# Top-k attention and a highway layer on one core: row maxima by a reduction of their own, one exponential for two rows of scores, and a sign change on GpSimd

## The chip, the core and the metric

The kernel runs on one NeuronCore of a Trainium2 chip. Its engines work side by side, each through its own queue in order, and wait for each other by semaphores: TensorE (PE), VectorE (DVE), ScalarE (ACT), GpSimd (POOL), and SyncE (SP), which here only starts DMAs. The metric is the device time of one execution in microseconds (us). Before the change the median of three runs is 804.51 us (803.33 to 804.64).

## The reference, cut to what matters

```python
def _attn_ref(q, k, v):                  # 8 batches, 8 heads, 576 rows, head size 64
    scores = (1 / sqrt(64)) * matmul(q, k.T)
    kth = the 32nd largest score of each row
    scores = where(scores >= kth, scores, -1e9)
    scores = scores - max(scores, axis=-1)
    attn = exp(scores)
    attn = attn / (sum(attn, axis=-1) + 1e-09)
    return matmul(attn, v)

def _moe_ref(x, w_h, w_t, b_t):          # 4608 tokens, width 512
    H = maximum(x @ w_h, 0.0)
    T = 1 / (1 + exp(-(x @ w_t + b_t)))
    return T * H + (1 - T) * x
```

The output of the attention, with the heads side by side, is the input `x` of the highway layer. All inputs and the output are float32; q, k and v are drawn with a deviation of 0.1.

## The kernel before

A unit is 128 rows of scores, each 576 columns wide: one block of 128 query rows of one head, or, for the last 64 rows of a sequence, two heads side by side. A batch has 4 x 8 + 4 = 36 units. Units are taken two at a time, so there are 18 pairs in a batch and 144 in all (`NG`). In 16 of the 18 pairs both units are whole blocks of one query range; in the other 2 each unit holds two half blocks.

`step(i)` writes out by hand, under a manual schedule, what each engine gets for pair i; the order of the calls is the order in each engine's queue. A pair lives over several steps:

- `scores` (L297): PE computes the scores of a pair in PSUM (two buffers of three banks). `copy_scores` (L347): ACT copies both units to SBUF as `sc`.
- `segments` (L352): DVE finds the 8 largest of each of 6 segments of 96 columns, 12 MAX8 a pair, into `cand`, sorted within a segment.
- `refine` (L359) finds the 24th largest candidate, a threshold, without sorting all 48. It takes neighbouring segments in opposite order: `high` (L367) is the pairwise maximum, `low` (L369) the pairwise minimum, `neg` (L371) is `high` with its sign changed. The 8 largest of `low` (L374) and of `neg` (L377) go into `en`, L379 combines them into column 1 of `cand`, and one reduction (L383) takes the maximum of column 0 (the row's largest score, `TOP`) and of column 1 (the threshold, `THR`) for both units into `wall`. `refine` is a generator: each `next(ra)` in `step` issues one of its instructions, so that others can be put between them.
- `biases` (L391): POOL multiplies the row maxima and the previous pair's kth values by constants: the biases of the exponential and of `above`.
- `mask_count` (L396): ACT writes a mask of the scores above the threshold and counts them; `mask_add` (L408): PE adds the mask to the scores in PSUM, which takes the counted ones out of the way; `below` (L423): DVE finds the 8 largest of what is left (L424).
- `hits` (L427, DVE), `pick_a` (L438, POOL) and `pick_b` (L442, DVE) choose by the count which of the nine values (threshold and the 8 below it) is the 32nd largest, into `wall`.
- `expo` (L415): ACT computes the exponential of a unit, with the row's maximum as its bias; two a pair, one on each side of the copy of the next pair's scores.
- `above` (L445, ACT) and `above_one` (L448, POOL) turn the kth value into a factor `r`; `keep_both` (L459, DVE) takes the minimum of `e` and `r` for both units; a DMA transposes the result (`transposes`, L486), PE multiplies by the values and a column of twos (`values`, L494), so the denominators come out with the sums.
- `ffn_pieces` (L556): when all heads of a query block are there, POOL adds a small constant to the denominators (L564), DVE takes the reciprocal (L566), POOL scales (L571), PE, ACT and POOL do the highway layer in pieces that later steps work off (`pool_work`, L617, L618, L631). `blk_norm` (L647) does the same in the tail.

At the end `finish` (L954) checks by three sums of signs that the assumptions held (`sure`, L943); if one does not hold, a slow loop computes everything again.

In a step DVE's queue after the 12 segment maxima of the next pair and the two maxima of L424 is: high, low, hits, neg, two maxima of low, two maxima of neg, `pick_b`, L379, the reciprocal if there is one, L383, `keep_both`. POOL's queue is: biases, `above_one`, a piece of the highway layer, `pick_a`, the sum of denominators if there is one, and the issue of a DMA. The biases of a step are made to wait for `keep_both` (`after`, L475).

Of the kernel before, what the change touches and what calls it, by code (L numbers as in the profile page):

```python
# [26 lines left out]
def kernel(  # L27
# [70 lines left out]

    TOP, THR, KTH = 0, 1, NPK + 1
    wall = consts.tile([P, NU + 2, NPK + 2], FP32)  # L100
    fac = consts.tile([P, 2, 2], FP32)
    nc.vector.memset(fac[:, :, 0], -scale)
    nc.vector.memset(fac[:, :, 1], -BIGK * (1.0 - 2.0**-24))
    be = consts.tile([P, NG + 1, 2, 2], FP32)
    NE = 4
# [5 lines left out]
    csum = consts.tile([P, NU], FP32)  # L111
    eps = consts.tile([P, H], FP32)
    nc.vector.memset(eps[:], 2.0e-9)
    nc.vector.memset(wall[:, 0:2, KTH : KTH + 1], 0.0)

    def kth(u):
        return wall[:, u + 2, KTH : KTH + 1]

    def tb(u):
        return be[:, u // 2, u % 2, 0:1]  # L120

    def eb(u):
        return be[:, u // 2 + 1, u % 2, 1:2]
# [223 lines left out]
    def copy_scores(both):  # L347
        sc = scpool.tile([P, 2, S], FP32, name="sc")
        nc.scalar.copy(sc[:], both)  # L349
        return [sc[:, s, :] for s in range(2)]  # L350

# [6 lines left out]

    def refine(g, cand):  # L359
        u0, u1 = pairs[g][0], pairs[g][1] + 1  # L360
# [6 lines left out]
        nc.vector.tensor_tensor(high[:].rearrange("p (s k r) -> p s k r", s=2, r=8), one, two, ALU.max)  # L367
        yield
        nc.vector.tensor_tensor(low[:].rearrange("p (s k r) -> p s k r", s=2, r=8), one, two, ALU.min)  # L369
        yield  # L370
        nc.vector.tensor_scalar(neg[:], high[:], -1.0, None, ALU.mult)  # L371
        yield
        for s in range(2):
            nc.vector.max(en[:, 0, s, 1:9], low[:, s * HALF : (s + 1) * HALF])  # L374
            yield
        for s in range(2):
            nc.vector.max(en[:, 1, s, 0:8], neg[:, s * HALF : (s + 1) * HALF])  # L377
            yield
        nc.vector.scalar_tensor_tensor(  # L379
            out=cand[:, :, :, 1], in0=en[:, 1, :, 0:8], scalar=-1.0, in1=en[:, 0, :, 0:8], op0=ALU.mult, op1=ALU.min  # L380
        )
        yield
        nc.vector.tensor_reduce(  # L383
            wall[:, u0:u1, TOP : THR + 1],
            cand[:, :, :, 0:2].rearrange("p s r k -> p s k r"),
            mybir.AxisListType.X,
            ALU.max,
        )
        yield

    def biases(g):  # L391
        return nc.gpsimd.tensor_tensor(be[:, g], wall[:, 2 * g : 2 * g + 2, TOP : KTH + 1 : KTH - TOP], fac[:], ALU.mult)  # L392

    def mask_count(u, ps):  # L396
        m1 = masks[u % NM]
        nc.scalar.activation(  # L398
            m1[:].bitcast(I8)[:, 1 : 2 * S : 2],
            ps,  # L400
            AF.Sign,
            bias=wall[:, u, THR : THR + 1],
            scale=ABOVE,
            accum_out=csum[:, u : u + 1],
        )
        return m1
# [8 lines left out]
    def expo(u, sc, e):  # L415
        nc.scalar.activation(e, sc, AF.Exp, bias=tb(u), scale=scale)  # L416
        return e

    def pair_tile(name):
        t = epool.tile([P, 2, S], BF16, name=name)  # L420
        return [t[:, s, :] for s in range(2)] + [t]

    def below(u, ps):  # L423
        nc.vector.max(wall[:, u, THR + 1 : KTH], ps)  # L424

# [12 lines left out]
    def pick_a(pair, hit):  # L438
        u0, u1 = pair[0], pair[1] + 1
        nc.gpsimd.tensor_tensor(hit[:], hit[:], wall[:, u0:u1, THR:KTH], ALU.mult)  # L440

    def pick_b(pair, hit):  # L442
        nc.vector.tensor_reduce(wall[:, pair[0] + 2 : pair[0] + 4, KTH], hit[:], mybir.AxisListType.X, ALU.add)

# [110 lines left out]

    def ffn_pieces(b, qt, xs):  # L556
        nh, ng, w = shape_of(qt)
# [3 lines left out]
        def norm():  # L561
            xs3 = xs[:, 0 : nh * DE].rearrange("p (h e) -> p h e", e=DE)
            rinv = cpool.tile([P, H], FP32, name="rinv")
            nc.gpsimd.tensor_tensor(rinv[:, 0:nh], xs3[:, :, D], eps[:, 0:nh], ALU.add)  # L564
            yield
# [81 lines left out]
    def blk_norm(k):  # L647
        nh, ng, w = shape_of(k["qt"])
        xs3 = k["xs"][:, 0 : nh * DE].rearrange("p (h e) -> p h e", e=DE)
        k["x"] = xpool.tile([P, dm], FP32, name="x")  # L650
        rinv = cpool.tile([P, H], FP32, name="rinv")
        nc.vector.tensor_tensor(rinv[:, 0:nh], xs3[:, :, D], eps[:, 0:nh], ALU.add)
# [55 lines left out]
    layers = []  # L708
    norms = []
    st = {}  # L710
# [19 lines left out]
    def start_scores(g):  # L730
        b = units[pairs[g][0]][0]
        for u in pairs[g]:
            for h in units[u][2]:
                ensure_prep(b, h // 2)
        st[g] = dict(ps=scores(pairs[g], preps[b]), sc=[None, None], et=[None, None], e=[None, None])
        st[g]["seg"] = 0
        st[g]["cand"] = cands[g % len(cands)]
# [5 lines left out]
    def segs(g, n):  # L743
        if g >= NG:
            return
        for c in range(st[g]["seg"], min(2 * NSEG, st[g]["seg"] + n)):
            s, k = divmod(c, NSEG)
            segments(st[g]["cand"][:, s], st[g]["ps"][s], k, k + 1)
        st[g]["seg"] += n
# [12 lines left out]
    def back_xs(g):  # L762
# [8 lines left out]
        if units[pairs[g][1]][2][-1] == H - 1:  # L771
            norms.append(ffn_pieces(b, qt, xs_t[b, qt]))

# [8 lines left out]
    def step(i):  # L782
# [32 lines left out]
        if late:  # L815
            late.pop(0)()
        if back:
            back_pv(j)
# [117 lines left out]
    signs = consts.tile([P, NU], BF16)  # L936
    cnt = consts.tile([P, 3], FP32)
    edge = consts.tile([P, 3], FP32)
    for j, e in enumerate((-(2.0**-60), 2.0**26, -(2.0**-100))):
        nc.vector.memset(edge[:, j : j + 1], e)  # L940
    flag = consts.tile([1, 1], I32)

    def sure(j, src, scale):  # L943

        nc.scalar.activation(
            signs[:],
            src,
# [6 lines left out]
    def finish():  # L954
# [7 lines left out]
        def xs_of(qt, h0, n):  # L962
# [3 lines left out]
            po["t"] = pso_tile()  # L966
            return dict(b=B - 1, qt=qt, xs=xs_t[B - 1, qt])

# [26 lines left out]
        below(pr[1], cur["ps"][1])  # L995
        cur["e"] = pair_tile("e")
        for s, u in enumerate(pr):
            expo(u, cur["sc"][s], cur["e"][s])
        x1 = xps.tile([P, 3 * BANK], FP32, tag="x", name="xs")
# [7 lines left out]
        old["et"] = transposes(pu[0])  # L1007
        nc.vector.tensor_tensor(hit[:], hit[:], wall[:, pr[0] : pr[1] + 1, THR:KTH], ALU.mult)
        pick_b(pr, hit)
# [3 lines left out]
        for s, home in enumerate((bank(x2, 1), bank(x1, 0))):  # L1013
# [5 lines left out]
            nc.scalar.copy(cur["et"][s].rearrange("p c q -> p (c q)"), turned)  # L1019
        sure(0, wall[:, 2 : NU + 2, KTH], 1.0)  # L1020
        sure(1, wall[:, 0:NU, TOP], -1.0)
        values_of(i - 1, 0)
# [5 lines left out]
        do_work(nc.vector, NG * dm)  # L1028
        nc.vector.scalar_tensor_tensor(cond[:], wall[:, 0:NU, THR + 1], ABOVE, wall[:, 0:NU, THR], ALU.mult, ALU.add)
        while stores:  # L1030
# [10 lines left out]
        project(bg, yb["qt"], yb["xT"], wt, True)  # L1041
        for j in range(3):
            nc.tensor.matmul(po["t"][0:1, 0:1], cnt[:, j : j + 1], ones[:], start=(j == 0), stop=(j == 2))
        blk_diff(ya, bank(x1, 0))
        store(*blk_out(ya))
        blk_gate(yb, bg)
        nc.vector.tensor_scalar(flag[:], po["t"][0:1, 0:1], 3.0 * P * NU - 0.5, None, ALU.is_ge)
        blk_diff(yb, bank(x2, 0))
# [103 lines left out]
```

## Time and profile before

| | value |
|---|---|
| median of three runs | 804.51 us |
| the profiled execution | 803.52 us |
| its span from the first to the last instruction | 801.9 us |
| TensorE clock granted | 0.997 |
| instructions | 20159 |

The profile page and the views drawn from the trace are of that one execution, and a term worked out from them is set against its 803.52 us. A row of a group reads: line, engine, operation, what it writes and reads with shapes, count, then busy time in us and the mean of one in ns, then the engine's idle time before these instructions in us and what ended it. A row of the timeline reads: start in us, duration in us, engine, line, operation. A row of the waits reads: who waited, for whom, total us, how many times, the longest. A row of the windows reads: the stretch in us, its length, then busy us and instruction count of PE, of PE's weight loads, of DVE, ACT and POOL, then clock, DMA share and GB/s. The line numbers are those of the kernel before.

### The profile page before, as it was taken

The page shows a single profiled execution, that of the slowest core. Times are in us where ns is not written, and L with a number is a line of the kernel's source. Part 1 is how long each engine was busy: PE and PEld are TensorE (multiplying, and loading weights), DVE is VectorE, ACT ScalarE, POOL GpSimd, SP SyncE. Part 2 cuts the span into 40 slices and gives each one's busy share as a digit, 9 for nine tenths or more (in the row PEclk, how much of TensorE's full clock was granted, in tenths as well). Part 3 has the DMA queues.
Part 4 walks back from the last instruction along what each step waited for, and adds up shares of the span by engine and source line. Part 5 has one row for each costly group of instructions (what it writes and reads, how often), then busy time and mean ns, then how long its engine had stood idle before and what let it go on. Part 6 is the DMA issues. An engine that isn't in the chain of part 4 may idle for free.

```text
span 801.9 us, 20159 instructions
## 1 busy us (share of the span) xinstructions
PE 685.3 (85%) x6369; PEld 494.0 (62%) x6459; DVE 768.5 (96%) x3846; ACT 759.3 (95%) x1401; POOL 564.9 (70%) x750
## 2 busy tenths in 40 slices
PE   7888988888988888888988889888898888988884
PEld 5666666566656666566665656656666566666662
DVE  6999999999999999999999999999999999999996
ACT  5999999999999999999999999999999999999984
POOL 2666867777777776787767776778777777766760
PEclk9999999999999999999999999999999999999998
DMA  6689977976799667987569766897677976565553
GB/s 122 87 134 166 130 118 133 161 128 96 138 153 148 110 98 132 155 144 115 99 137 166 119 114 112 150 151 130 111 125 134 167 117 108 95 104 108 112 84 90
DMA packets 341779, 100.31 MB, mean 125 GB/s; under 512 B 326048, under 2 KB 333856, under 8 KB 341664
## 3 DMA queue, kind: packets, MB, share of 16 engines
q1 hardware_dynamic: 286448, 79.14, 51.8%
q0 software_dynamic: 53536, 19.34, 22.2%
q8 instruction: 53, 0.87, 0.4%
q10 hardware_dynamic: 1680, 0.46, 0.3%
q14 instruction: 62, 0.51, 0.2%
HBM read 31.72 MB, written 9.44 MB: 51 GB/s over the span
## 4 chain that ended last, share of the span: by engine, by line
DVE 65%; ACT 15%; PE 12%; DMA 3%; issue 3%; SPq 1%; DVEq 0%; ACTq 0%
DVE cand L354 24%; DVE wall L424 19%; DVE ep L463 8%; ACT m L398 5%; PE xs L327 4%; ACT e L416 3%; ACT sc L349 3%; DMA xT<-xb 2%; DVE en L374 2%; DVE en L377 2%; DVE cand L379 2%; PE fp L529 2%; ACT r L446 2%; DVE high L367 2%; PE pso L279 2%
## 5 line engine op out<-in xcount | busy, mean ns | idle before, releaser
L354 DVE MAX8 cand<-xs 128x8 f32<-128x96 f32 x1728 | 297.0, 247 | 9.7 <-PE xs L336 6.5
L279 PE MATMUL pso<-cst,ident_b 128*128 128x252 bf16 x1841 | 246.8, 272 | 41.9 <-ACT xs L515 39.5
L449 POOL TENSOR_SCALAR r<-sc,wall 128x576 bf16<-128x576 f32 x135 | 232.5, 1722 | 0.0
L416 ACT ACTIVATE e<-sc,be 128x576 bf16<-128x576 f32 x288 | 227.8, 791 | 0.1
L279 PEld LDWEIGHTS <-ident_b 128*128 128x128 bf16 x1841 | 173.5, 98 | 80.6 <-issue 48.7
L424 DVE MAX8 wall<-xs 128x8 f32<-128x576 f32 x288 | 203.9, 749 | 5.1 <-PE xs L411 2.5
L310 PE MATMUL xs<-kT,qT 64*128 64x256 f32 x1024 | 145.3, 400 | 37.2 <-DVE high L367 28.4
L349 ACT COPY sc<-xs 128x1152 f32<-128x1152 f32 x144 | 161.5, 1122 | 1.0 <-DVE cand L354 0.9
L310 PEld LDWEIGHTS xs<-kT,qT 64*128 64x128 f32 x1024 | 93.0, 186 | 68.6 <-issue 40.2
L398 ACT ACTIVATE m<-xs,wall 128x576 int8<-128x576 f32 x144 | 108.0, 750 | 11.0 <-DVE wall L383 9.4
L398 ACT ACTIVATE m<-sc,wall 128x576 int8<-128x576 f32 x144 | 112.4, 780 | 0.0
L440 POOL TENSOR_TENSOR hit<-hit,wall 128x18 f32<-128x18 f32 x143 | 32.1, 225 | 113.5 <-DVE hit L430 113.5
L446 ACT ACTIVATE r<-sc,be 128x576 bf16<-128x576 f32 x143 | 110.8, 775 | 0.0
L463 DVE TENSOR_TENSOR ep<-e,r 128x1152 bf16<-128x1152 bf16 x135 | 100.9, 748 | 0.4 <-ACT e L416 0.4
L411 PE MATMUL xs<-m,ident_b 128*128 128x512 bf16 (+1 forms) x512 | 90.6, 274 | 9.1 <-ACT m L398 7.0
L392 POOL TENSOR_TENSOR be<-wall,fac 128x4 f32<-128x4 f32 x144 | 29.0, 201 | 78.1 <-DVE ep L463 56.4
L501 PEld LDWEIGHTS <-et 128*128 128x128 bf16 (+1 forms) x1600 | 68.6, 100 | 19.9 <-issue 3.5
L501 PE MATMUL pso<-vb,et 128*128 128x65 bf16 (+1 forms) x1600 | 74.4, 194 | 4.9 <-DMA et<-ep 1.0
L411 PEld LDWEIGHTS <-ident_b 128*128 128x128 bf16 x576 | 51.0, 98 | 35.0 <-issue 13.8
L319 PEld LDWEIGHTS xs<-kd,qT 128*128 128x128 f32 x256 | 38.1, 188 | 42.5 <-issue 42.1
L319 PE MATMUL xs<-kd,qT 128*128 128x128 f32 x256 | 62.5, 326 | 0.0
L618 POOL TENSOR_TENSOR h<-h,x 128x512 f32<-128x512 f32 (+1 forms) x37 | 43.0, 1161 | 0.6
(128 smaller groups left out, 992.6 us busy)
## 6 DMA issues: line engine op xcount, KB each, us to landing
kin<-in_k_dram SPq DMA_DIRECT2D x64, 128.0 KB, 3.1
qin<-in_q_dram SPq DMA_DIRECT2D x62, 128.0 KB, 3.1
out_dram<-s SPq DMA_DIRECT2D x30, 256.0 KB, 3.2
s<-h POOLq DMA_DIRECT2D x29, 256.0 KB, 3.7
xb<-x POOLq DMA_DIRECT2D x30, 128.0 KB, 2.6
vb<-in_v_dram POOLq DMA_DIRECT2D x28, 128.0 KB, 3.9
et<-ep SPq DMA_TRANSPOSE x143, 3.9
vb<-in_v_dram POOLq DMA_DIRECT2D x24, 64.0 KB, 3.2
```

Of the source, the lines that this page charges most:

```text
L279: nc.tensor.matmul(po["t"][:, 4 * DE : BANK], ident_b[:], cst[:, 0 : BANK - 4 * DE], start=True, stop=True, skip_group_check=True,)
L310: nc.tensor.matmul(ps[:, mo + n0 : mo + n0 + 256], qT[r : r + D, hp, qs : qs + P], kT[r : r + D, hp, n0 : n0 + 256], start=(n0 == 0), stop ...
L349: nc.scalar.copy(sc[:], both)
L354: nc.vector.max(cand[:, s, :], sc[:, s * SEG : (s + 1) * SEG])
L398: nc.scalar.activation(m1[:].bitcast(I8)[:, 1 : 2 * S : 2], ps, AF.Sign, bias=wall[:, u, THR : THR + 1], scale=ABOVE, accum_out=csum[:, u ...
L411: nc.tensor.matmul(ps[:, s0:s1], ident_b[:], m1[:, s0:s1], start=False, stop=True, skip_group_check=True)
L416: nc.scalar.activation(e, sc, AF.Exp, bias=tb(u), scale=scale)
L424: nc.vector.max(wall[:, u, THR + 1 : KTH], ps)
L446: nc.scalar.activation(r, sc, AF.Relu, bias=eb(u), scale=BIGK)
L449: nc.gpsimd.tensor_scalar(r, sc, kth(u), None, ALU.is_ge)
L463: return nc.vector.tensor_tensor(out, e[:], r[:], ALU.min)
L501: nc.tensor.matmul(pso[r0 : r0 + ql, col : col + DE], ets[s][:, c, gi * P2 : gi * P2 + ql], vb[:, h, vc, :], start=(c == 0), stop=(c == nc ...
```

## The change

Three things change together, and the values they need move with them.

1. `neg`, the pairwise maxima with their sign changed, is computed by GpSimd as a product with a tile of -1 (`minus`), directly after `high`; VectorE's L371 is gone, and `hits` follows `low` as before.
2. The reduction L383 becomes two. One takes, in one instruction with three overlapping ranges over `cand` (which has two more blocks, filled with -3e38), the row maximum of the first unit, of both units together (`PEAK`), and of the second unit. The other takes the two thresholds. `wall` is laid out by pairs.
3. In the joint pairs (the 16 of 18 with whole blocks) one exponential covers both units, 1152 columns, with the shared maximum `PEAK` as its bias. Since a row's exponentials are then scaled down by exp(row maximum - PEAK), the constant added to its denominator is scaled alike: POOL computes the distances (`distances`) for eight units at a time, ACT their exponential (`share`), 32 of each, and `denominators` adds it. The other 16 pairs keep two exponentials, now both ahead of the copy of scores, and get a bias tile of their own from one more POOL product. The end has a fourth check: no row maximum lies more than 40 (in the exponent) below its pair's.

The diff, cut to its core:

```diff
     cands = []
     for i in range(4):
-        cand = consts.tile([P, 2, 8, 8], FP32, name=f"cand{i}")
-        nc.vector.memset(cand[:, :, NSEG:, 0:1], -3.0e38)
+        cand = consts.tile([P, 4, 8, 8], FP32, name=f"cand{i}")
+        nc.vector.memset(cand[:, 0 :: 3, 0:NSEG, 0:1], -3.0e38)
...
         nc.vector.tensor_tensor(high[:].rearrange("p (s k r) -> p s k r", s=2, r=8), one, two, ALU.max)
         yield
+        nc.gpsimd.tensor_tensor(neg[:], high[:], minus[:], ALU.mult)
+        yield
         nc.vector.tensor_tensor(low[:].rearrange("p (s k r) -> p s k r", s=2, r=8), one, two, ALU.min)
-        yield
-        nc.vector.tensor_scalar(neg[:], high[:], -1.0, None, ALU.mult)
         yield
...
-        nc.vector.tensor_reduce(
-            wall[:, u0:u1, TOP : THR + 1],
-            cand[:, :, :, 0:2].rearrange("p s r k -> p s k r"),
-            mybir.AxisListType.X,
-            ALU.max,
+        at = cands4[:]
+        heads = bass.AP(tensor=at.tensor, offset=at.offset, ap=[at.ap[0], [64, 3], [64, 2], [8, NSEG]])
+        nc.vector.tensor_reduce(wall[:, g, 0:LIST], heads, mybir.AxisListType.XY, ALU.max)
+        yield
+        nc.vector.tensor_reduce(lists(g)[:, :, 0], cand[:, :, :, 1], mybir.AxisListType.X, ALU.max)
+        yield
+
+    def joint(g):
+        return units[pairs[g][0]][1] < nfull
...
     def biases(g):
-        return nc.gpsimd.tensor_tensor(be[:, g], wall[:, 2 * g : 2 * g + 2, TOP : KTH + 1 : KTH - TOP], fac[:], ALU.mult)
+        if not joint(g):
+            nc.gpsimd.tensor_tensor(bs[:, g % 4], wall[:, g, 0:LIST:2], fat[:], ALU.mult)
+        return nc.gpsimd.tensor_tensor(be[:, g], wall[:, g, PEAK : KTH + LW + 1 : LW], fac[:], ALU.mult)
+
+    def distances(g):
+        g0 = g + 1 - NP
+        nc.gpsimd.tensor_tensor(
+            dist[:, g0 : g + 1],
+            wall[:, g0 : g + 1, 0:LIST:2],
+            wall[:, g0 : g + 1, PEAK].unsqueeze(2).to_broadcast([P, NP, 2]),
+            ALU.subtract,
         )
+        share = cpool.tile([P, H], FP32, name="share")
+
+        def expo_share():
+            nc.scalar.activation(
+                share[:], dist[:, g0 : g + 1].rearrange("p g s -> p (g s)"), AF.Exp, bias=eps[:, 0:1], scale=scale
+            )
+
+        return share, expo_share
...
+    def exponentials(g):
+        e = pair_tile("e")
+        sc = st[g]["sc"]
+        if joint(g):
+            nc.scalar.activation(e[2][:], sc[2], AF.Exp, bias=be[:, g, 0:1], scale=scale)
+        else:
+            for s, u in enumerate(pairs[g]):
+                expo(u, sc[s], e[s])
+        return e
...
+        while lows:
+            lows.pop(0)()
         if back:
             back_pv(j)
             back_xs(j)
...
         if live:
-            st[i]["e"] = pair_tile("e")
-            expo(pr[0], st[i]["sc"][0], st[i]["e"][0])
+            st[i]["e"] = exponentials(i)
         if nxt:
             copy_both(i + 1)
...
         if live:
-            expo(pr[1], st[i]["sc"][1], st[i]["e"][1])
+            pass
...
-        for _ in range(2):
+        for _ in range(3):
             next(ra, None)
         if live:
             hit = hits(pr)
             pick_a(pr, hit)
+            shared(i)
             scaling = norms.pop(0)() if norms else iter(())
             next(scaling, None)
...
-        for _ in range(5):
+        for _ in range(4):
             next(ra, None)
         if live:
             pick_b(pr, hit)
         next(ra, None)
         if live:
             next(scaling, None)
         for _ in ra:
             pass
         last = masked()
```

DVE's queue in a step is then: high, low, hits, two maxima of low, two maxima of neg, `pick_b`, L379, the reciprocal if there is one, the reduction for the maxima, the reduction for the thresholds, `keep_both`. POOL's is: biases, `above_one`, a piece of the highway layer, neg, `pick_a`, the distances or the sum of denominators if there is one, the issue of a DMA. PE's instructions and their order are unchanged but for one more check matmul at the end.

More of the change, by code (lines that the diff above doesn't have):

```diff
@@ L1 @@
+import math
 from contextlib import ExitStack
@@ L97 @@
         nc.vector.memset(pidx[:, jj : jj + 1], S - 2.0 * (TOP_K - jj))
[L99 to L104, printed above, removed]
+    LIST, LW = 3, NPK + 2
+    PEAK, KTH = 1, LIST + NPK
+    wall = consts.tile([P, NG + 1, LIST + 2 * LW - 1], FP32)
+    fac = consts.tile([P, 3], FP32)
+    nc.vector.memset(fac[:, 0:1], -scale)
+    nc.vector.memset(fac[:, 1:3], -BIGK * (1.0 - 2.0**-24))
+    fat = consts.tile([P, 2], FP32)
+    nc.vector.memset(fat[:], -scale)
+    be = consts.tile([P, NG + 1, 3], FP32)
+    bs = consts.tile([P, 4, 2], FP32)
+    dist = consts.tile([P, NG, 2], FP32)
+    nc.gpsimd.memset(dist[:], 0.0)
     NE = 4
@@ L349, in copy_scores @@
         nc.scalar.copy(sc[:], both)
-        return [sc[:, s, :] for s in range(2)]
+        return [sc[:, s, :] for s in range(2)] + [sc[:]]
     def segments(cand, sc, lo, hi):
@@ L357, with refine @@
     HALF = NSEG // 2 * 8
-    def refine(g, cand):
-        u0, u1 = pairs[g][0], pairs[g][1] + 1
+    def refine(g, cands4):
+        cand = cands4[:, 1:3]
         en = ends[g % NE]
@@ L382, in refine, with biases, shared @@
         yield
-        nc.vector.tensor_reduce(
-            wall[:, u0:u1, TOP : THR + 1],
-            cand[:, :, :, 0:2].rearrange("p s r k -> p s k r"),
-            mybir.AxisListType.X,
-            ALU.max,
-        )
-        yield
-    def biases(g):
-        return nc.gpsimd.tensor_tensor(be[:, g], wall[:, 2 * g : 2 * g + 2, TOP : KTH + 1 : KTH - TOP], fac[:], ALU.mult)
+        at = cands4[:]
[6 more added lines that the diff above has]
+        return units[pairs[g][0]][1] < nfull
+    def biases(g):
+        if not joint(g):
[8 more added lines that the diff above has]
+            ALU.subtract,
+        )
+        share = cpool.tile([P, H], FP32, name="share")
[4 more added lines that the diff above has]
+        return share, expo_share
+    def shared(g):
+        if joint(g) and units[pairs[g][1]][2][-1] == H - 1:
+            share, ex = distances(g)
+            shares.append(share)
+            lows.append(ex)
     def mask_count(u, ps):
@@ L401, in mask_count @@
             AF.Sign,
-            bias=wall[:, u, THR : THR + 1],
+            bias=top9(u, 0, 1),
             scale=ABOVE,
@@ L423, in below @@
     def below(u, ps):
-        nc.vector.max(wall[:, u, THR + 1 : KTH], ps)
+        nc.vector.max(top9(u, 1), ps)
     def hits(pair):
@@ L439, in pick_a @@
         u0, u1 = pair[0], pair[1] + 1
-        nc.gpsimd.tensor_tensor(hit[:], hit[:], wall[:, u0:u1, THR:KTH], ALU.mult)
+        nc.gpsimd.tensor_tensor(hit[:], hit[:], lists(u0 // 2), ALU.mult)
     def pick_b(pair, hit):
-        nc.vector.tensor_reduce(wall[:, pair[0] + 2 : pair[0] + 4, KTH], hit[:], mybir.AxisListType.X, ALU.add)
+        nc.vector.tensor_reduce(wall[:, pair[0] // 2 + 1, KTH : KTH + LW + 1 : LW], hit[:], mybir.AxisListType.X, ALU.add)
     def above(u, sc, r):
@@ L554, with denominators, ffn_pieces @@
     blocks = []
-    def ffn_pieces(b, qt, xs):
+    def denominators(e, rinv, sums, share):
+        if share is None:
+            return e.tensor_scalar(rinv, sums, 2.0e-9, None, ALU.add)
+        return e.tensor_tensor(rinv, sums, share[:], ALU.add)
+    def ffn_pieces(b, qt, xs, share=None):
         nh, ng, w = shape_of(qt)
@@ L563, in norm @@
             rinv = cpool.tile([P, H], FP32, name="rinv")
-            nc.gpsimd.tensor_tensor(rinv[:, 0:nh], xs3[:, :, D], eps[:, 0:nh], ALU.add)
+            denominators(nc.gpsimd, rinv[:, 0:nh], xs3[:, :, D], share)
             yield
@@ L651, in blk_norm @@
         rinv = cpool.tile([P, H], FP32, name="rinv")
-        nc.vector.tensor_tensor(rinv[:, 0:nh], xs3[:, :, D], eps[:, 0:nh], ALU.add)
+        denominators(nc.vector, rinv[:, 0:nh], xs3[:, :, D], k["share"])
         nc.vector.reciprocal(rinv[:, 0:nh], rinv[:, 0:nh])
@@ L708 @@
     layers = []
-    norms = []
+    norms, shares, lows = [], [], []
     st = {}
@@ L734, in start_scores @@
                 ensure_prep(b, h // 2)
-        st[g] = dict(ps=scores(pairs[g], preps[b]), sc=[None, None], et=[None, None], e=[None, None])
+        st[g] = dict(ps=scores(pairs[g], preps[b]), sc=[None, None, None], et=[None, None], e=[None, None])
         st[g]["seg"] = 0
@@ L771, in back_xs @@
         if units[pairs[g][1]][2][-1] == H - 1:
-            norms.append(ffn_pieces(b, qt, xs_t[b, qt]))
+            norms.append(ffn_pieces(b, qt, xs_t[b, qt], shares.pop(0) if joint(g) else None))
     late = []
@@ L936 @@
     signs = consts.tile([P, NU], BF16)
-    cnt = consts.tile([P, 3], FP32)
-    edge = consts.tile([P, 3], FP32)
-    for j, e in enumerate((-(2.0**-60), 2.0**26, -(2.0**-100))):
+    cnt = consts.tile([P, 4], FP32)
+    edge = consts.tile([P, 4], FP32)
+    for j, e in enumerate((-(2.0**-60), 2.0**26, -(2.0**-100), 40.0 / scale)):
         nc.vector.memset(edge[:, j : j + 1], e)
@@ L966, in xs_of @@
             po["t"] = pso_tile()
-            return dict(b=B - 1, qt=qt, xs=xs_t[B - 1, qt])
+            share = shares.pop(0) if qt < nfull else None
+            return dict(b=B - 1, qt=qt, xs=xs_t[B - 1, qt], share=share)
         def masked(unit, s, of):
@@ L995, in finish @@
         below(pr[1], cur["ps"][1])
-        cur["e"] = pair_tile("e")
-        for s, u in enumerate(pr):
-            expo(u, cur["sc"][s], cur["e"][s])
+        cur["e"] = exponentials(i)
         x1 = xps.tile([P, 3 * BANK], FP32, tag="x", name="xs")
@@ L1007, in finish @@
         old["et"] = transposes(pu[0])
-        nc.vector.tensor_tensor(hit[:], hit[:], wall[:, pr[0] : pr[1] + 1, THR:KTH], ALU.mult)
+        nc.vector.tensor_tensor(hit[:], hit[:], lists(i), ALU.mult)
         pick_b(pr, hit)
@@ L1028, in finish @@
         do_work(nc.vector, NG * dm)
-        nc.vector.scalar_tensor_tensor(cond[:], wall[:, 0:NU, THR + 1], ABOVE, wall[:, 0:NU, THR], ALU.mult, ALU.add)
+        for s in range(2):
+            c = LIST + s * LW
+            nc.vector.scalar_tensor_tensor(
+                cond[:, s::2], wall[:, 0:NG, c + 1], ABOVE, wall[:, 0:NG, c], ALU.mult, ALU.add
+            )
         while stores:
@@ L1041, in finish @@
         project(bg, yb["qt"], yb["xT"], wt, True)
-        for j in range(3):
-            nc.tensor.matmul(po["t"][0:1, 0:1], cnt[:, j : j + 1], ones[:], start=(j == 0), stop=(j == 2))
+        for j in range(4):
+            nc.tensor.matmul(po["t"][0:1, 0:1], cnt[:, j : j + 1], ones[:], start=(j == 0), stop=(j == 3))
         blk_diff(ya, bank(x1, 0))
```

33 lines of the change are left out of this document (22 added, 11 removed).

## The prediction

> **What bounds the kernel now.** I read the page first: busy shares, then the chain that ended last.
>
> ```profile
> PE 685.3 (85%) x6369; PEld 494.0 (62%) x6459; DVE 768.5 (96%) x3846; ACT 759.3 (95%) x1401; POOL 564.9 (70%) x750
> DVE 65%; ACT 15%; PE 12%; DMA 3%; issue 3%; SPq 1%; DVEq 0%; ACTq 0%
> ```
>
> Two engines look full, DVE at 96% and ACT at 95%, and shares cannot say which of them sets the pace. The chain gives DVE 65% and ACT 15%. The table of windows cuts off the first 20 us and the tail:
>
> ```profile
> 20.00:780.00 760.00, 659.28 (x6148) 475.91 (x6234) 743.03 (x3732) 738.16 (x1361) 557.95 (x732) 1.00 0.76 126
> ```
>
> In the 760 us between, the third busy column (DVE) has 743.0: only 17 us of idle time. The fourth (ACT) has 738.2. The view of waits then tells who was late for whom:
>
> ```profile
> DVE cand L354 <- PE xs L336: 6.5, 15, 0.5
> DVE cand L354 <- PE xs L319: 2.9, 7, 0.6
> DVE wall L424 <- PE xs L411: 2.5, 3, 1.1
> DVE ep L463 <- ACT e L416: 0.4, 2, 0.2
> ACT m L398 <- DVE wall L383: 9.4, 25, 0.7
> ```
>
> DVE waited for ACT itself 0.4 us in all; its waits are for score matmuls (6.5 and 2.9 us, L336 and L319), which start when DVE's own `below` is through, and for mask matmuls (2.5 us, L411), which do stand behind ACT's masks. So a pair costs what DVE's queue costs, and I follow DVE's queue. One pair in the timeline, with the POOL instruction inside it:
>
> ```profile
> 408.84 0.19 DVE L367 TENSOR_TENSOR high<-cand 128x48 f32<-128x48 f32 x1
> 408.94 0.20 DVE L369 TENSOR_TENSOR low<-cand 128x48 f32<-128x48 f32 x1
> ...
> 409.06 0.17 DVE L430 TENSOR_TENSOR hit<-pidx,csum 128x18 f32<-128x18 f32 x1
> ...
> 409.15 0.18 DVE L371 TENSOR_SCALAR neg<-high 128x48 f32<-128x48 f32 x1
> 409.24 0.26 DVE L374 MAX8 en<-low 128x8 f32<-128x24 f32 x2
> 409.31 0.23 POOL L440 TENSOR_TENSOR hit<-hit,wall 128x18 f32<-128x18 f32 x1 [1.63 <-DVE hit L430]
> 409.43 0.25 DVE L377 MAX8 en<-neg 128x8 f32<-128x24 f32 x2
> 409.60 0.15 DVE L443 TENSOR_REDUCE wall<-hit 128x2 f32<-128x18 f32 x1
> 409.71 0.19 DVE L379 SCALAR_TENSOR_TENSOR cand<-en 128x16 f32<-128x16 f32 x1
> 409.93 0.21 DVE L383 TENSOR_REDUCE wall<-cand 128x4 f32<-128x32 f32 x1
> 410.06 0.75 DVE L463 TENSOR_TENSOR ep<-e,r 128x1152 bf16<-128x1152 bf16 x1
> ```
>
> What matters here is starts, not durations: `low` starts 0.10 after `high` though `high` lasts 0.19, so independent instructions overlap by about 0.08. Only where one needs the last one's result does it wait: `wall` (L383) starts 0.03 after the end of `cand` (L379), 0.22 after its start. Counting from `high`, the starts are: low 0.10, hit 0.22, neg 0.31, maxima of low 0.40, maxima of neg 0.59, the sum of hits (L443) 0.76, L379 0.87, L383 1.09, keep 1.22. These 1.22 us, 144 times, are what the change edits.
>
> **Part 1: the sign change goes to POOL (144 pairs).** Removing L371 frees one start-to-start step, 409.24 - 409.15 = 0.09, but the maxima of low need `low` (end 0.30), so they come at 0.34 and the maxima of neg could start at 0.52 instead of 0.59. They now wait for POOL. `high` ends at 0.19; POOL answers a DVE result 0.08 later (hit ends at 409.23, POOL starts at 409.31), so neg starts at 0.27. No trace shows a 48-element product on POOL; the neighbours:
>
> ```profile
> L440 POOL TENSOR_TENSOR hit<-hit,wall 128x18 f32<-128x18 f32 x143 | 32.1, 225 | 113.5 <-DVE hit L430 113.5
> L618 POOL TENSOR_TENSOR h<-h,x 128x256 f32<-128x256 f32 x7 | 5.1, 726 | 0.5
> L571 POOL TENSOR_TENSOR x<-xs,rinv 128x512 f32<-128x512 f32 x31 | 32.3, 1043 | 0.0
> L571 POOL TENSOR_TENSOR x<-xs,rinv 128x256 f32<-128x256 f32 x7 | 4.2, 603 | 0.0
> ```
>
> From 225 at 18 elements to 726 at 256 is 2.1 ns an element: 288 ns at 48. The product with a broadcast (603 at 256, 1043 at 512: 1.72 an element) gives 246, the lower bound. I take 0.29, as the row of 18 is nearest: neg ends at 0.56. POOL's way back is at most 0.06 (L440 ends at 409.54, L443 starts at 409.60); I take 0.05. Maxima of neg then start at 0.60-0.61, L379, which needs their end (+0.085 +0.17 +0.03), at 0.88 instead of 0.87. Behind neg on POOL stands the product of hits (L440): it starts at 0.52 instead of 0.47, ends at 0.75, and L443 comes at 0.80, which still lets L379 start on time. So without contention this part costs +0.01 a pair, by the short duration -0.03. That POOL is free when `high` ends is in the row of L440: 113.5 us of idle before 143 of them, 0.8 each.
>
> Contention is the open price L. The trace shows it in one direction, with a reciprocal in the same pair:
>
> ```profile
> 283.10 1.27 POOL L617 TENSOR_TENSOR s<-h,x 128x512 f32<-128x512 f32 x1 [0.48 <-ACT h L616]
> ...
> 283.85 0.58 DVE L367 TENSOR_TENSOR high<-cand 128x48 f32<-128x48 f32 x1
> ...
> 285.12 0.19 DVE L379 SCALAR_TENSOR_TENSOR cand<-en 128x16 f32<-128x16 f32 x1
> 285.21 0.20 DVE L566 RECIPROCAL rinv<-rinv 128x8 f32<-128x8 f32 x1
> 285.34 0.21 DVE L383 TENSOR_REDUCE wall<-cand 128x4 f32<-128x32 f32 x1
> ```
>
> `high`, with two inputs in SBUF, took 0.58 instead of 0.19: it ended 0.06 after POOL's instruction (284.37), so it was locked out until then. In the changed order `hit`, again with two inputs, runs from 0.22 to 0.39 while neg wants to start at 0.27. Bounds: L = 0 if hit's reads are through before neg asks, 0.13 if neg gets nothing before hit's end (0.39 - 0.27 = 0.13 by unrounded times). I take 0.04: `high` needed only 0.06 once it had the port, so `hit` holds it for a small part of its 0.17. Part 1: +0.05 a pair, bounds -0.03 and +0.14.
>
> The Trainium skill, "SBUF — State Buffer", section "Who interferes with whom", states that a DVE instruction with two SBUF inputs and a GpSimd one that reads SBUF share a port, and that the first to issue keeps it for the whole instruction. The stretched `high` agrees; no row shows POOL locked out by DVE. Taken at its word for `hit` it makes L 0.13, which is rival B.
>
> **Part 2: the row maxima get a reduction of their own.** L383 with four results becomes one with three (before it) and one with two.
>
> ```profile
> L383 DVE TENSOR_REDUCE wall<-cand 128x4 f32<-128x32 f32 x144 | 30.3, 210 | 3.6
> L443 DVE TENSOR_REDUCE wall<-hit 128x2 f32<-128x18 f32 x144 | 22.0, 153 | 0.0
> L566 DVE RECIPROCAL rinv<-rinv 128x8 f32<-128x8 f32 x31 | 6.1, 195 | 0.0
> L566 DVE RECIPROCAL rinv<-rinv 128x4 f32<-128x4 f32 x7 | 1.2, 171 | 0.0
> ```
>
> The new one reads column 0 of the candidates, which L379 does not write, so it goes into the 0.22 in which L383 waits for L379, as the reciprocal does above (0.09 after L379, and L383 still 0.22 after it). About as long as L383 (0.21, so a step of 0.13), it lets the second start at 0.22 to 0.25: +0.015. Its cover is that gap; without it the step costs 0.13. The second reduction has L443's shape nearly (0.15 against 0.21), so keep follows 0.07 after it, not 0.13: -0.057. Net -0.04 a pair (bounds -0.06 and 0.00, if results don't shorten it). In the 38 pairs with a reciprocal (31 + 7) the gap is taken: +0.12 x 38 = +4.6 us (bounds 0 and 5).
>
> **Part 3: one exponential a pair.** 128 of 144 pairs are joint.
>
> ```profile
> L416 ACT ACTIVATE e<-sc,be 128x576 bf16<-128x576 f32 x288 | 227.8, 791 | 0.1
> L349 ACT COPY sc<-xs 128x1152 f32<-128x1152 f32 x144 | 161.5, 1122 | 1.0 <-DVE cand L354 0.9
> L515 ACT COPY xs<-pso 128x260 f32<-128x260 f32 x72 | 27.6, 383 | 9.7 <-PE pso L501 7.4
> ```
>
> From 383 at 260 columns to 1122 at 1152 is 0.83 ns a column, so one of 1152 is 791 + 576 x 0.83 = 1269 against 1582: 0.31 x 128 = 40 us off ACT. The 32 new small exponentials give back at most 32 x 0.38 = 12. Some 30 us leave ACT, but only DVE's waits can shrink: the 17 us of idle, less 9.4 for the scores, leave about 7. Most of that has PE held by other work, so I take -2.5 (bounds 0 and -7). The score copy moves behind the longer exponential, 0.48 later; the masks queued behind it on ACT come earlier, since the second exponential is gone.
>
> **Part 4: the rest.** An extra POOL product ahead of L449 in 16 pairs, differences in 32 (some 0.2 each), a fourth check in the tail. They lie in POOL's idle time; +0.8 (bounds 0 and 3).
>
> **Sum** on the profiled run's own time of 803.5 (span 801.9): parts 1 and 2, 144 x (0.05 - 0.04) = +1.6; reciprocals +4.6; ACT -2.5; rest +0.8: +4.5, so 808.0. The median of the runs is 1.0 above the profiled run: 809.
>
> **Rivals.**
> A, it ends faster: neg takes 246 ns and L is 0. Part 1 is -0.03, 144 x -0.07 = -10 us, and with +2.9 of the rest the sum is -7: 797. For it: POOL's product with a broadcast. Against: 225 ns already at 18 elements. It decides from a neg that is back before 0.57.
> B, `hit` keeps the port and neg waits: L = 0.13, 144 x 0.10 = +14.5, +2.9: 822. For it: the lock in the row of `high`. Against: the lock's holder there was a 1.27 us POOL instruction, not a short DVE one. If neg takes the port between `low` and `hit` instead, `hit` ends 0.06 after neg at 0.62, POOL's product of hits at 0.92, L443 comes at 0.97 and L379 at 1.04: +0.17 - 0.04, 144 times, 19 us: 826.
> C, ACT was the bound after all: DVE's idle in the middle goes, 17 us in place of the 2.5 of part 3: 809 - 14.5 = 794. Against: 0.4 us of DVE waits on ACT.
> D, a row maximum lies more than 40 in the exponent below its pair's, the flag is not set and the slow loop runs: at least double the time, over 1600. With inputs drawn at 0.1 the scores lie far closer together.
>
> **How the numbers follow.** Forecast 0.52 (its own range 804 to 817); A 0.24; B 0.18; C 0.05; D 0.01. The predicted time is the forecast's. The range of 797 to 826 takes in A and B. From no change this kernel can be told by about 0.2% (1.6 us). Faster: all of C and most of A, 0.28; same: the lower edge of the forecast and a part of A, 0.12; slower: 0.60.
>
> **What would show it.** Maxima of neg start about 0.64 after `high` and wait for POOL (right), or at 0.52 with no wait (A), or 0.7 and later (B); `hit` longer than 0.17 says neg took the port. L383's successor pair starts 0.09 and 0.22 after L379, and keep 0.07 after the second. ACT's share falls by 3 to 4 points without DVE's idle time falling likewise. Wrong would be: DVE's share falling while the time falls too, or a wait for POOL on another instruction than the maxima of neg or L443.

## The result, and the profile after

The changed kernel is slower by 0.35%: over 20 runs of each, 805.96 us against 803.15 us, a ratio of 1.0035 (95% interval 1.0027 to 1.0043). The three runs shown ahead of the prediction had lain 1.4 us above the longer series of the kernel before.

The page of the changed kernel, its first block and the shares of the chain that ended last:

```profile
span 803.8 us, 20357 instructions
PE 690.8 (86%) x6461; PEld 493.6 (61%) x6461; DVE 775.5 (96%) x3850; ACT 742.3 (92%) x1307; POOL 612.7 (76%) x943
DVE 71%; PE 12%; ACT 10%; DMA 3%; issue 2%; SPq 0%; POOL 0%; DVEq 0%; ACTq 0%
```

The table of windows without the first 20 us and the tail (after PE and PE's weight loads come DVE, ACT and POOL):

```profile
20.00:780.00 760.00, 663.11 (x6217) 474.40 (x6216) 747.45 (x3723) 718.97 (x1261) 604.16 (x920) 1.00 0.76 126
```

ACT has become 19 us emptier in these 760 us (738.2 before), and DVE is busy 4.4 us longer (743.0 before). The view of waits says where ACT's time went:

```profile
ACT m L445 <- DVE wall L406: 30.7, 68, 1.0
DVE cand L373 <- PE xs L355: 6.4, 16, 0.5
DVE cand L373 <- PE xs L338: 2.6, 6, 0.8
DVE wall L481 <- PE xs L458: 3.9, 6, 1.0
```

ACT's masks now wait 30.7 us for DVE's thresholds, 9.4 before. DVE's own waits for scores (6.4 and 2.6) are what they were (6.5 and 2.9), and its wait for masks (3.9, 2.5 before) is no shorter. The relief of ACT went into ACT's own idle time.

One pair of the changed kernel in the timeline, the same one as before the change:

```profile
408.93 0.19 DVE L386 TENSOR_TENSOR high<-cand 128x48 f32<-128x48 f32 x1
409.04 0.20 DVE L390 TENSOR_TENSOR low<-cand 128x48 f32<-128x48 f32 x1
...
409.15 0.17 DVE L487 TENSOR_TENSOR hit<-pidx,csum 128x18 f32<-128x18 f32 x1
409.20 0.29 POOL L388 TENSOR_TENSOR neg<-high,minus 128x48 f32<-128x48 f32 x1 [1.41 <-DVE high L386]
409.27 0.27 DVE L393 MAX8 en<-low 128x8 f32<-128x24 f32 x2
409.44 0.23 POOL L497 TENSOR_TENSOR hit<-hit,wall 128x18 f32<-128x18 f32 x1
409.52 0.27 DVE L396 MAX8 en<-neg 128x8 f32<-128x24 f32 x2
409.70 0.17 DVE L500 TENSOR_REDUCE wall<-hit 128x2 f32<-128x18 f32 x1
409.82 0.19 DVE L398 SCALAR_TENSOR_TENSOR cand<-en 128x16 f32<-128x16 f32 x1
409.91 0.21 DVE L404 TENSOR_REDUCE wall<-cand 128x3 f32<-128x36 f32 x1
410.04 0.18 DVE L406 TENSOR_REDUCE wall<-cand 128x2 f32<-128x16 f32 x1
410.14 0.75 DVE L520 TENSOR_TENSOR ep<-e,r 128x1152 bf16<-128x1152 bf16 x1
```

From the start of `high`: neg on POOL 0.27, maxima of low 0.34, maxima of neg 0.59, sum of hits 0.77, L398 0.89, the two reductions 0.98 and 1.11, keep 1.21. Before, the maxima of neg came at 0.59 too, L379 at 0.87 and keep at 1.22. The instruction taken off DVE has freed nothing: the maxima of neg start 0.03 after POOL is done (409.20 + 0.29 = 409.49), so the step that was saved turned into a wait. The front half, up to L398, is 0.02 longer, since the two maxima of neg together take 0.27 and took 0.25 before (409.43, L377); the back half is 0.03 shorter.

A pair with a reciprocal, the same as the one shown before, from L398 on:

```profile
284.82 0.19 DVE L398 SCALAR_TENSOR_TENSOR cand<-en 128x16 f32<-128x16 f32 x1
284.91 0.19 DVE L629 RECIPROCAL rinv<-rinv 128x8 f32<-128x8 f32 x1
285.02 0.16 DVE L404 TENSOR_REDUCE wall<-cand 128x3 f32<-128x36 f32 x1
285.11 0.17 DVE L406 TENSOR_REDUCE wall<-cand 128x2 f32<-128x16 f32 x1
285.19 0.75 DVE L520 TENSOR_TENSOR ep<-e,r 128x1152 bf16<-128x1152 bf16 x1
```

Here the gap behind L398 is taken by the reciprocal, and the extra reduction costs a step: 0.37 from L398 to keep, 0.34 before (285.12 to 285.46, where keep stands in the timeline of the kernel before):

```profile
285.46 0.75 DVE L463 TENSOR_TENSOR ep<-e,r 128x1152 bf16<-128x1152 bf16 x1
```

### The profile page after: what moved, and what is told of

It is laid out like the page before. It is cut to its first block, busy times and chain, and to the rows that moved or that the text cites. A ratio compares the mean times of both kernels' runs of the same rounds, so it can differ in the third digit from the quotient of the medians.

```text
span 803.8 us, 20357 instructions
## 1 busy us (share of the span) xinstructions
PE 690.8 (86%) x6461; PEld 493.6 (61%) x6461; DVE 775.5 (96%) x3850; ACT 742.3 (92%) x1307; POOL 612.7 (76%) x943
## 4 chain that ended last, share of the span: by engine, by line
DVE 71%; PE 12%; ACT 10%; DMA 3%; issue 2%; SPq 0%; POOL 0%; DVEq 0%; ACTq 0%
DVE cand L373 26%; DVE wall L481 21%; DVE ep L520 8%; PE xs L346 4%; ACT m L445 3%; DVE en L396 3%; DVE en L393 3%; DMA xT<-xb 2%; PE fp L586 2%; PE pso L298 2%; DVE cand L398 2%; DVE high L386 2%; DVE low L390 2%; ACT sc L368 1%; PE xs L329 1%
## 5 line engine op out<-in xcount | busy, mean ns | idle before, releaser
L470 ACT ACTIVATE e<-sc,be 128x1152 bf16<-128x1152 f32 x128 | 161.0, 1258 | 0.1
L445 ACT ACTIVATE m<-xs,wall 128x576 int8<-128x576 f32 x144 | 107.5, 747 | 32.3 <-DVE wall L406 30.7
L388 POOL TENSOR_TENSOR neg<-high,minus 128x48 f32<-128x48 f32 x144 | 41.1, 285 | 92.4 <-DVE high L386 89.9
L458 PE MATMUL xs<-m,ident_b 128*128 128x512 bf16 (+1 forms) x576 | 103.2, 285 | 5.5 <-ACT m L445 3.4
L416 POOL TENSOR_TENSOR be<-wall,fac 128x3 f32<-128x3 f32 x144 | 28.3, 197 | 58.7 <-DVE ep L520 49.3
```

What stands on the lines that cost most here:

```text
L445: nc.scalar.activation(m1[:].bitcast(I8)[:, 1 : 2 * S : 2], ps, AF.Sign, bias=top9(u, 0, 1), scale=ABOVE, accum_out=csum[:, u : u + 1],)
L458: nc.tensor.matmul(ps[:, s0:s1], ident_b[:], m1[:, s0:s1], start=False, stop=True, skip_group_check=True)
L470: nc.scalar.activation(e[2][:], sc[2], AF.Exp, bias=be[:, g, 0:1], scale=scale)
```

## The experiments

Times are medians of 11 or 12 runs, of 5 where that is said, and of 2 for the slowest version. Each ratio is to the kernel before, run on the same chip, with its 95% interval; it can differ from the quotient of the two medians shown by up to 0.0009, and differences in us are taken from the ratios. Where two ratios are set against each other, each brings its interval, mostly of about 0.001 up and down. Diffs are against the kernel before or the changed one, as named, and cut to what matters (`...`).

**Part 1 undone in the changed kernel.**

```diff
-        nc.gpsimd.tensor_tensor(neg[:], high[:], minus[:], ALU.mult)
-        yield
         nc.vector.tensor_tensor(low[:]..., one, two, ALU.min)
         yield
+        nc.vector.tensor_scalar(neg[:], high[:], -1.0, None, ALU.mult)
+        yield
...
```

The counts of `next(ra)` in `step` go back with it, so that neg stands behind `hits` again.

> The changed kernel with part 1 undone: neg is computed by DVE again, in its old place after hits. Theory (the DVE queue sets the pace, and the way over POOL costs it 0.02 us a pair: in the changed kernel L398 starts 0.89 after high, before 0.87): 144 x 0.02 = 3 us less than the changed kernel, a ratio to before of 0.998 to 1.000. Rival (part 1 is free and the extra reduction, the reciprocals behind it or the moved exponentials cost the 0.35%): the ratio stays at 1.003 to 1.004.

803.06 us against 802.76, ratio 1.0004 (0.9994 to 1.0013): just above the range that was expected, and clear of the rival's. Nearly all of the 0.35% goes with part 1: 1.0035 - 1.0004, some 2.5 us (1 to 4 by the ends of the two intervals). The rest of the change together shows no gain, although it takes 34 us of exponentials off ACT (by the groups of the changed kernel 161.0 for the joint ones, 23.0 for the others and 9.5 for the small ones, against 227.8).

**Part 1 alone in the kernel before** (the same lines the other way).

> The kernel before with part 1 alone. Theory: the maxima of neg wait for POOL and start later than DVE's own queue would let them, and L379 comes 0.02 to 0.03 us later: +3 to +4 us, a ratio of 1.004 to 1.005. Rival (the saved DVE instruction pays for the way over POOL): 0.999 to 1.001. A lock of hit or neg would show as hit over 0.18 us or neg over 0.30.

804.43 us against 802.76, 1.0020 (1.0010 to 1.0030), between the two ranges: slower, as the theory has it, but at half of its size. The groups by line and form of this run, POOL's neg and then DVE's instructions around it:

```profile
L371 POOL TENSOR_TENSOR neg<-high,minus 128x48 f32<-128x48 f32 x144 | 41.4, 287 | 91.1 <-DVE high L369 88.3 <-DVE low L373 1.4
...
L376 DVE MAX8 en<-low 128x8 f32<-128x24 f32 x288 | 39.1, 177 | 0.0
L379 DVE MAX8 en<-neg 128x8 f32<-128x24 f32 x288 | 39.1, 177 | 0.1
L432 DVE TENSOR_TENSOR hit<-pidx,csum 128x18 f32<-128x18 f32 x144 | 24.2, 168 | 0.0
```

`hit` lasts 168 ns (170 before) and neg 287: neither was held by the other. The maxima last 177 ns; with neg on DVE, in the run above this one, the same two groups read:

```profile
L393 DVE MAX8 en<-low 128x8 f32<-128x24 f32 x288 | 37.5, 170 | 0.0
L396 DVE MAX8 en<-neg 128x8 f32<-128x24 f32 x288 | 35.8, 164 | 0.0
```

The view of waits hardly shows the stall (0.1 us of idle time), since the engine counts as busy with the maxima of low while the next instruction is held. It has to be read from starts.

**POOL's answer made later**: in the changed kernel neg goes behind the product of hits in POOL's queue.

```diff
-        for _ in range(3):
+        for _ in range(2):
             next(ra, None)
         if live:
             hit = hits(pr)
             pick_a(pr, hit)
+            next(ra, None)
             shared(i)
...
```

In `refine`, neg stands behind `low` for this.

> The changed kernel with POOL's neg placed behind the product of hits on POOL instead of ahead of it. Theory (the maxima of neg wait for POOL, and every ns there goes into the pair): neg starts 0.66 after high instead of 0.27, the maxima of neg at 0.98 instead of 0.59, +0.39 x 144 = 56 us, less some 8 us that waits for scores take in: 845 to 865 us. Rival (the wait is covered by later waits): under 815 us.

849.72 us against 804.01, 1.0574 (1.0555 to 1.0593), inside the expected range: 43 us more than the changed kernel. A pair of this run, with the wait that now shows:

```profile
401.20 0.19 DVE L386 TENSOR_TENSOR high<-cand 128x48 f32<-128x48 f32 x1
...
401.68 0.23 POOL L497 TENSOR_TENSOR hit<-hit,wall 128x18 f32<-128x18 f32 x1 [1.02 <-DVE hit L487]
401.86 0.29 POOL L390 TENSOR_TENSOR neg<-high,minus 128x48 f32<-128x48 f32 x1
...
402.18 0.27 DVE L396 MAX8 en<-neg 128x8 f32<-128x24 f32 x2 [0.37 <-POOL neg L390]
```

The maxima of neg start 0.98 after `high`, 0.39 later than in the changed kernel, and 43 us are 0.30 a pair: three quarters of this delay on POOL went into the time. This place has no slack; the changed kernel stands with POOL's answer just beyond its edge.

**Part 2 alone, in its plain form**: two reductions of two results each.

```diff
-        nc.vector.tensor_reduce(wall[:, u0:u1, TOP : THR + 1], cand[:, :, :, 0:2]..., X, ALU.max)
+        nc.vector.tensor_reduce(wall[:, u0:u1, TOP], cand[:, :, :, 0], X, ALU.max)
+        yield
+        nc.vector.tensor_reduce(wall[:, u0:u1, THR], cand[:, :, :, 1], X, ALU.max)
```

> The kernel before with part 2 alone: L383 becomes two reductions of two results each, for row maxima and for thresholds. Theory: the first goes into the gap behind L379, keep comes 0.03 sooner after the second in 106 pairs, and in the 38 pairs with a reciprocal the gap is taken, +0.05 each: -3 + 2 = -1 us, ratio 0.998 to 1.000. Rival (the extra instruction costs its own step of 0.10 to 0.13 in each pair): +14 to +19 us, 1.018 to 1.023.

801.00 us against 802.76, 0.9974 (0.9964 to 0.9984): one DVE instruction more a pair, and faster by 2.1 us, more than expected. The two pairs that show how, from the timeline of this run, without and with a reciprocal:

```profile
204.43 0.19 DVE L379 SCALAR_TENSOR_TENSOR cand<-en 128x16 f32<-128x16 f32 x1
204.52 0.17 DVE L383 TENSOR_REDUCE wall<-cand 128x2 f32<-128x16 f32 x1
204.65 0.18 DVE L385 TENSOR_REDUCE wall<-cand 128x2 f32<-128x16 f32 x1
204.75 0.75 DVE L460 TENSOR_TENSOR ep<-e,r 128x1152 bf16<-128x1152 bf16 x1
...
209.60 0.19 DVE L379 SCALAR_TENSOR_TENSOR cand<-en 128x16 f32<-128x16 f32 x1
209.69 0.20 DVE L563 RECIPROCAL rinv<-rinv 128x8 f32<-128x8 f32 x1
209.81 0.13 DVE L383 TENSOR_REDUCE wall<-cand 128x2 f32<-128x16 f32 x1
209.85 0.17 DVE L385 TENSOR_REDUCE wall<-cand 128x2 f32<-128x16 f32 x1
209.94 0.75 DVE L460 TENSOR_TENSOR ep<-e,r 128x1152 bf16<-128x1152 bf16 x1
```

The first reduction sits in the gap in which DVE waited for L379 anyway; the second starts 0.22 after L379, as the one reduction did, and keep follows 0.10 after it instead of 0.13. Even with a reciprocal in the gap it is 0.34 to keep, as before the change, where a loss of 0.05 was expected.

**Part 3 alone**: one exponential a joint pair, with the first unit's maximum as bias.

```diff
-            expo(pr[0], st[i]["sc"][0], st[i]["e"][0])
+            if units[pr[0]][1] < nfull:
+                nc.scalar.activation(st[i]["e"][2][:], st[i]["sc"][2], AF.Exp, bias=tb(pr[0]), scale=scale)
+            else:
...
-        if live:
-            expo(pr[1], st[i]["sc"][1], st[i]["e"][1])
```

> The kernel before with part 3 alone: one exponential for a joint pair, with the first unit's row maximum as the bias of both; the small constant in the denominators is not scaled for it. Theory (ACT stands off the path): ACT's busy time falls by some 40 us and the time stays, ratio 0.999 to 1.001; ACT's wait for DVE grows. Rival (the prediction's -2.5 us, bounds 0 and -7): 0.991 to 0.997.

802.59 us against 802.76, 0.9995 (0.9986 to 1.0005): no change that can be told. From the page and the waits of this run:

```profile
PE 684.5 (86%) x6369; PEld 494.0 (62%) x6459; DVE 768.9 (96%) x3846; ACT 737.6 (92%) x1273; POOL 564.9 (71%) x750
ACT m L398 <- DVE wall L383: 29.7, 71, 1.0
```

ACT is busy 22 us less (759.3 before) and waits 20 us more for DVE (9.4 before). Its busy time fell by less than the 40 us expected, since it counts overlapping instructions once: the exponentials' own groups fell by 44 us, from 227.8 to 160.8 (joint) and 23.0 (others).

**Part 3 undone in the changed kernel**, in its cost only: two exponentials with the shared bias.

```diff
-            nc.scalar.activation(e[2][:], sc[2], AF.Exp, bias=be[:, g, 0:1], scale=scale)
+            for s in range(2):
+                nc.scalar.activation(e[s], sc[s], AF.Exp, bias=be[:, g, 0:1], scale=scale)
```

> The changed kernel with part 3 undone in its cost only: a joint pair gets two exponentials of 576 columns again, both with the shared bias. Theory (ACT is off the path by the 31 us that it waits for DVE's thresholds in the changed kernel): ACT's busy time rises by some 40 us, its wait falls, and the time stays within 0.1% of the changed kernel's 1.0035. Rival (ACT's relief is worth 2.5 us or more): 1.0065 or more.

806.40 us against 804.01 over 5 runs, 1.0039 (1.0025 to 1.0052), against 1.0035 with one. ACT's wait for DVE's thresholds fell from 30.7 to 10.2 us. So in both directions, at an ACT share of 92% or 95%, the exponential decides nothing that these runs can tell.

**The three-range reduction narrowed**: neg on DVE, and in place of three maxima only the two units' own, the first serving as the shared one.

```diff
-        at = cands4[:]
-        heads = bass.AP(..., ap=[at.ap[0], [64, 3], [64, 2], [8, NSEG]])
-        nc.vector.tensor_reduce(wall[:, g, 0:LIST], heads, mybir.AxisListType.XY, ALU.max)
+        nc.vector.tensor_reduce(wall[:, g, PEAK:LIST], cand[:, :, 0:NSEG, 0], mybir.AxisListType.X, ALU.max)
...
```

> The changed kernel with neg on DVE again and the three-range reduction narrowed to two results: the first unit's row maximum serves as the shared one, the distances are taken from it, all else stays. Theory (the long reduction is dear where the reciprocal has taken the gap: L404 to L406 0.118 in the mean, against 0.109 with two results): 1.5 to 2 us under the run with neg on DVE (1.0004), ratio 0.998 to 0.999. Rival (the loss is in the distances, the small exponentials and the bias tile): it stays at 1.000.

802.20 us against 804.01, 0.9980 (0.9970 to 0.9989), where the three-range form gave 1.0004: some 1.9 us for the third range. The distances are taken from the first unit's maximum as well, so on these inputs this version does the work of the changed kernel, and it is faster than both kernels. It guards less: a distance can now be positive, when the second unit's maximum is the larger, and the fourth check looks only for distances below -40.

**Parts 2 and 3 in plain form together**, without distances and their small exponentials, the small constant in the denominators not scaled (the two diffs above, of part 2 alone and part 3 alone).

> The kernel before with parts 2 and 3 in a plain form: two reductions of two results each, one exponential a joint pair with the first unit's row maximum as bias, no three-range reduction, no distances; the small constant in the denominators is not scaled. Theory (the parts add up): the ratio of the run with two reductions alone, 0.9974, times that of one exponential alone, 0.9995: 0.996 to 0.998. Rival (together they lose what they gain alone, as in the changed kernel without part 1, 1.0004): 0.999 to 1.001.

800.94 us against 804.01 over 5 runs, 0.9964 (0.9950 to 0.9978): the parts add up. This is the lowest ratio of the versions tried, but its interval overlaps that of the two reductions alone (0.9974). The distances, the small exponentials and the bias tile then cost 0.9980 - 0.9964, some 1.3 us; the two intervals overlap, so that figure stays open.

## Why the prediction was right or wrong

The sign and the mechanism were right: DVE's queue sets the pace, the way over POOL ends just after DVE needs it, ACT's relief is not seen. The size was off: +4.5 us forecast, +2.8 us measured. The terms were further off than their sum, and it is luck that they nearly cancel: by the runs, part 1 was put some 4.7 us too dear and the others together some 3.6 us too cheap, with the 1.3 us left open above counted to part 4. (The first term of the sum, 144 x 0.01, is 1.4 and not 1.6.)

- **The mis-sized term is the contention L in part 1.** The prediction put 0.04 us a pair on neg waiting for the port that `hit` holds, 144 x 0.04 = 5.8 us. Measured: 0. POOL's neg started 0.27 after `high`, with 0.12 of `hit` still to run, and lasted 285 ns in the changed kernel, where 288 was expected without contention; `hit` lasted 172 (170 before). The maxima of neg came at 0.59, not at 0.64.

```profile
L388 POOL TENSOR_TENSOR neg<-high,minus 128x48 f32<-128x48 f32 x144 | 41.1, 285 | 92.4 <-DVE high L386 89.9 <-DVE low L390 1.4
L487 DVE TENSOR_TENSOR hit<-pidx,csum 128x18 f32<-128x18 f32 x144 | 24.7, 172 | 0.0
```

- **Part 1 without L** was put at +0.01 a pair and measured +0.02, from a cause that was not in the sum. The answer of POOL took 0.03, not 0.05, so the first maximum of neg starts as early as before the change, at 0.59. But behind the wait the two of them take 0.27 together and not 0.25 (177 ns each in the mean instead of 164 to 166), and L398 waits for the second. By the runs part 1 costs 2.5 us (with and without it in the changed kernel) or 1.7 us (alone); the forecast was 0.05 x 144 = 7.2.
- **Part 2** was forecast at -0.04 x 144 + 4.6 = -1.2 us. Its plain form gave -2.1 us, the third range took back some 1.9. Two figures in it were off and nearly cancelled, again by luck: keep follows 0.10 after the last reduction, not 0.07 (L406 lasts 0.18, not 0.15 as L443), and a reciprocal in the gap costs 0.03 in the pair shown, not 0.08 (0.12 - 0.04).
- **Part 3** was forecast at -2.5 us, by the part of DVE's idle time that stands behind ACT's masks. Measured: -0.4 us, inside the noise. DVE's waits for scores were the same before and in the run with one exponential (6.5 and 2.9 against 6.7 and 2.9 us), and its waits for masks are few in both (2.5 us in three, 1.0 us in one). The bound of 0 was right. What those waits for PE come from was not tested.
- **Part 4**, +0.8 us, was put into POOL's idle time. The traces show 0.7 us of it elsewhere, on an instruction that the prediction did not have. In the 7 pairs whose block holds four heads, POOL's sum of denominators (L616) starts 0.10 after the product of hits ends, where it had overlapped it before (L564), and the reciprocal comes 0.20 after L398 instead of 0.09 (414.90 to 414.99, L379). The first four lines are of the changed kernel, the last two of the kernel before:

```profile
414.63 0.22 POOL L497 TENSOR_TENSOR hit<-hit,wall 128x18 f32<-128x18 f32 x1
414.95 0.23 POOL L616 TENSOR_SCALAR rinv<-xs 128x4 f32<-128x4 f32 x1
415.01 0.19 DVE L398 SCALAR_TENSOR_TENSOR cand<-en 128x16 f32<-128x16 f32 x1
415.21 0.18 DVE L629 RECIPROCAL rinv<-rinv 128x4 f32<-128x4 f32 x1
...
414.69 0.20 POOL L564 TENSOR_TENSOR rinv<-xs,eps 128x4 f32<-128x4 f32 x1
414.99 0.17 DVE L566 RECIPROCAL rinv<-rinv 128x4 f32<-128x4 f32 x1
```

What changed for L616 is its form: a sum with a constant in place of a sum with a tile. The run with the narrowed reduction, where neg is on DVE, has the delay too (0.18 to 0.19 after L398), so it stands in the 1.3 us left open above. No run isolates it.

- **Rivals.** A was half right: L is 0, as it had it, but neg lasted 285 ns and not 246, and came too late to gain anything. Its sign, a neg back before 0.57, was drawn too loosely: POOL's record ends at 0.56 (409.49), and DVE starts on it only at 0.59. B is refuted by the durations of neg and `hit`. C is refuted twice, by the run with one exponential alone and by the one with two in the changed kernel. D did not happen.

## What to carry to other kernels

Where two engines show the same share of busy time, look at which of them waits for the other and price an edit in the starts of the one that doesn't wait; 22 us of busy time taken from the other engine brought nothing that could be measured here. An instruction moved off the full engine saves its step only if its result is back before the full engine's own next instruction could start: work out that moment from starts, with the neighbouring engine's way there and back. And a gap in which a queue waits for its own last result is room for an independent instruction: splitting one reduction in two, so that half went into the gap, gave the only gain of this change.

## What the runs showed of the hardware

DVE can hold up POOL too, but not every DVE instruction does in which POOL's record starts. In the changed kernel POOL's bias product for the pairs that are not joint falls into `keep_both`, a DVE instruction with two inputs in SBUF, and ends only after it (from the timeline, and the group of the 16 products by the view of one line):

```profile
195.34 0.75 DVE L520 TENSOR_TENSOR ep<-e,r 128x1152 bf16<-128x1152 bf16 x1
195.80 0.34 POOL L415 TENSOR_TENSOR bs<-wall,fat 128x2 f32<-128x2 f32 x1
...
L415 POOL TENSOR_TENSOR bs<-wall,fat x16: 240/460/740, 99.1 to 780.5; 128x2 f32<-128x2 f32 x16
```

In 14 of the 16 it ends 0.05 to 0.06 after keep does (here 196.14 against 196.09), whenever it began; it lasts 460 ns in the median where products of about its size take some 200 (197 for L416, 128x3). Yet neg, which by its record starts inside `hit`, loses nothing. The Trainium skill, "SBUF — State Buffer", section "Who interferes with whom", says the first to issue keeps the shared port for its whole instruction: the long `keep_both` agrees, the 18-column `hit` does not, if issue is read from the records. That POOL asks for the port only some time after its recorded start would explain both; no run here measures it, and that it is the port which held the product is argued from these ends, not tested.

A DVE instruction that starts on a result just finished can cost more than the wait. The maxima behind POOL's neg lasted 177 ns instead of 164 to 166, though they read and write the same shapes. It is not peculiar to POOL: the maxima of low, which in the changed order start 0.03 after `low` ends (409.04 + 0.20 against 409.27), also lasted 177 ns, and 170 where neg stood between. Nor is it POOL's work at the same time: where neg went behind the product of hits, and so started only after the maxima of low, these lasted 177 ns too. Why is open.
